# A planner with a pass backwards, a second split third of the last product, a shorter carry chain and one load for the first a

## The chip, the cores and the metric

One Trainium2 chip, one core of it. The metric is device microseconds of one execution, lower is better. A core has TensorE (PE in the rows; PEld is its weight loads), VectorE (DVE), ScalarE (ACT), GpSimd (POOL) and SyncE (SP, which here only issues transfers).

## The reference

Three stages, one after the other. A gated linear attention with a complex decay (batch 4, 8 heads, 768 steps, head size 48), a dense layer with a maximum of three products, and a mixture of 8 experts of which each token takes one:

```python
for t in range(S):
    new_re = ar * S_re - ai * S_im
    new_im = ar * S_im + ai * S_re
    S_re, S_im = (new_re + kv, new_im)
    y[:, :, t] = np.einsum('bhd,bhde->bhe', q[:, :, t], S_re)
...
h = np.maximum(np.maximum(x @ w1, x @ w2), x @ w3)     # 3072 x 384 by 384 x 768
x = h @ w_out                                           # 768 x 384
...
expert_idx = np.argmax(logits, axis=1)                  # logits: normed x by normed embeddings / tau
out[mask] = gate_w[mask, None] * (np.maximum(x[mask] @ w1[e], 0.0) @ w2[e])
```

## The kernel before

The program has two phases. Phase 1 computes attention and the dense layer; phase 2 the experts. The change touches phase 1 only.

**Phase 1** runs over 12 units of 256 tokens. Each unit u goes through: `load_a` (decays, 768 KB), `front` (norms the decays, L438 to L462), `mid` (running products of the decays: 7 steps over the 8 lanes, then the "carry chain" over 8 blocks and 3 groups, with the small tiles `Ct`, `gt`, `G` and `C`, L471 to L513), `back` (scales q and k into `QK` and sends them by 12 transfers `S<-QK` into the tile S, L515 to L564), `attn` for two halves (TensorE: pk, pa, pT, py; L582 to L657) and `moe1` (L769 to L822). A step of `mid` is `cmul_step`: one multiply (`sa`, `sb`, `sc`) and one add, each depending on the one before. `mid` ends with a sign change (`minus`) that the carry chain needs, two memsets into `Ct`, one copy into it, and the same again for `G`.

**moe1** has three thirds f2 = 0, 1, 2. For each, 54 matmuls into three PSUM tiles `ph`, a maximum on VectorE giving `h` (128 x 512), and the last product h by `w_out` into `px`. In thirds below `SPLIT` (1, L1065) h and the weight are split in a high and a low part (`hhi`, `hlo`; `wohi`, `wolo`) and px takes three fp32r matmuls a product; in the others px takes one fp32 matmul, which the trace shows as two instructions. `hhi` has one buffer, the tag "h" (h and hlo) has two.

**Weights** (L660 to L754): 24 pieces of 64-bit weights come through the POOL queue, are turned to fp32 on ScalarE and VectorE and, where they are needed split, split with two ScalarE casts and two matmuls (`pd`). This runs beside the first unit.

**What sets the order.** Every instruction of phase 1 goes through a `Recorder` (L125 to L320), which knows a cost for each and the dependences; `issue` (L247) sorts them by a list schedule: it takes the engine that is free first, and of the instructions that could start within `SLACK` = 120 ns the one with the smallest key, then the longest path behind it. Keys are given by hand (`KEYS`, L1070): a unit's number plus an offset, so that routing (`route_early`, key 10.5) lies between `moe1(10)` (10.3) and `moe1(11)` (11.3). Instructions of one engine run in the order of this plan. All recorded instructions stand at L313 in the trace. The plan also puts filler matmuls (`keep_warm`, L571; trace line L578) ahead of TensorE work where it foresees an idle time over 0.9 us.

**Into phase 2.** `route_early` (L939) chooses experts for the first 20 tiles: VectorE work, two small matmuls `within` in the middle of it, more VectorE work, a table `tab` with the experts of the first blocks; then `first_rows` (L988) gathers the first block's tokens and transposes them. Phase 2 then loads the first expert's weights (`queue_q_buf`, L1177), copies them (`w1s`, L1206) and multiplies (`ph<-xT,w1s`, L1252). None of phase 2 is known to the planner.

Of the kernel before, what the change touches and what calls it, by code (L numbers as in the profile page):

```python
# [31 lines left out]
L = 8  # L32
# [84 lines left out]
class Op:  # L117
    __slots__ = ("eng", "calls", "cost", "preds", "succs", "rank", "n", "start", "end", "dma", "key")

    def __init__(self, eng):  # L120
        self.eng, self.calls, self.cost, self.preds, self.dma = eng, [], 0.0, {}, 0.0
        self.succs, self.key = [], 0.0


class Recorder:  # L125
# [6 lines left out]
    def __init__(self, nc):  # L132
        self.nc = nc
        self.ops = []
        self.hist = {}
        self.slot = {}
        self.before = {}
        self.cur = None
        self.idle = None
        self.lazy = None  # L140
# [49 lines left out]
    def price(self, op, eng, method, out, ins, k):  # L190
        n = out.free_size()
        psum = any(x.space == PSUM for x in ins + [out])
        if "dma" in method:
            op.cost += 1040.0 if eng != "sync" else 460.0 if len(ins[0].shape) < 4 or ins[0].space == bass.MemoryType.DRAM else 625.0
            op.dma = 2000.0 + out.nbytes() / 200.0
        elif eng == "tensor":
            m, r, b = ins[0].free_size(), ins[0].dtype == F32R, ins[0].dtype == BF16
            op.cost += (14.0 if r else 2.5) + (2 * n if method == "transpose" else n if r else max(n, m) if b else 4 * max(n, m)) / 2.4 * (
                0.25 if m <= 32 else 0.6 if m <= 64 else 1.0)
            if m <= 32 and len(op.calls) == 1:  # L200
                op.cost += 250.0
        elif eng == "vector":
            w = 0.5 if method in ("tensor_copy", "tensor_scalar", "memset") and not psum else 8 if method == "reciprocal" else 1
            op.cost += (n * w + 66) / 0.96
        elif eng == "scalar":
            op.cost += (144 if isinstance(k.get("scale"), bass.AP) else 51 if psum else 94) + n / 1.2
            op.cost += 100 * (k.get("accum_out") is not None) + 90 * isinstance(k.get("bias"), bass.AP)
        else:
            op.cost += 150 + n * 2.2 if method in ("tensor_mul", "tensor_sub") else 100 + n / 0.9
# [36 lines left out]

    def issue(self):  # L247
        ops = self.ops
        for i, o in enumerate(ops):
            o.n = len(o.preds)  # L250
            for p, raw in o.preds.items():
                p.succs.append((o, raw))
        done = set()
        for o in reversed(ops):
            o.rank = o.cost + max((self.lat(o, s, raw) + s.rank for s, raw in o.succs), default=0.0)
        free = dict.fromkeys(("vector", "scalar", "tensor", "gpsimd", "sync"), 0.0)
        ready = {e: [] for e in free}
        for o in ops:
            o.start = 0.0
            if o.n == 0:  # L260
                ready[o.eng].append(o)
        left = len(ops)
        for e, x in self.START.items():
            free[e] = x
        pipe = 0.0
# [20 lines left out]
        while left:  # L286
            best = None
            for e, row in ready.items():
                if not row:
                    continue  # L290
                t = max(free[e], min(o.start for o in row))
                if best is None or t < best[0]:
                    best = t, e
            t, e = best
            o = max((o for o in ready[e] if o.start <= t + self.SLACK), key=lambda o: (-o.key, o.rank))
            if o.key == self.lazy:
                o = max((x for x in ready[e] if x.start <= t + 130.0 and x.key < o.key), key=lambda o: (-o.key, o.rank), default=o)
            ready[e].remove(o)
            o.start = max(o.start, t)
            if e == "tensor":  # L300
                x = free[e]
                while self.idle and x > self.IDLE[0] and o.start - x > self.IDLE[1] and self.idle(o):
                    x = hold(x, 2 * 216.0)
                    x += self.IDLE[2] if warm[0] else 50.0
                o.end = free[e] = hold(o.start, o.cost)
            else:
                o.end = free[e] = o.start + o.cost
            if o.dma:

                pipe = max(pipe, o.end) + o.dma - 2000.0  # L310
                o.dma = pipe + 2000.0 - o.end
            for c in o.calls:
                getattr(getattr(self.nc, c[0]), c[1])(*c[2], **c[3])  # L313
            left -= 1
            for s, raw in o.succs:
                s.start = max(s.start, o.end + self.lat(o, s, raw))
                s.n -= 1
                if s.n == 0:
                    ready[s.eng].append(s)
        return max(o.end for o in ops)  # L320

    START = {"gpsimd": 4000.0, "scalar": 2500.0, "sync": 1000.0}
# [5 lines left out]
class Prog:  # L328
# [64 lines left out]
    def consts2(self):  # L393
# [13 lines left out]
        q.sync.dma_start(self.rtau, self.io["tau"].to_broadcast([128, 1]))  # L407
        with self.keyed(self.KEYS["early"]):
            q.vector.reciprocal(self.rtau, self.rtau)
# [54 lines left out]
    def cmul_step(self, out, f, x, shape, tag):  # L464
# [4 lines left out]
        v.tensor_add(out, m[:, 0], m[:, 1])  # L469

    def mid(self, u):  # L471
# [5 lines left out]
        for i in range(1, L):  # L477
            self.cmul_step(X[:, 1:3, i], X[:, 1:3, i - 1], X[:, :, i], [NB], "sa")

        Ct = self.tl(p, [128, 3, NB], "Ct", 1, f"Ct{u}")  # L480
# [7 lines left out]
        minus(tot[:, 0], tot[:, 2], 1)  # L488
# [3 lines left out]
        v.memset(Cg[:, 1, :, 0], 1.0)  # L492
        v.memset(Cg[:, 2, :, 0], 0.0)
        v.tensor_copy(Cg[:, 1:3, :, 1], Tg[:, 1:3, :, 0])
        gt = self.tl(p, [128, 3, 12], "gt", 1, f"gt{u}")
        for i in range(2, 9):
            out = Cg[:, 1:3, :, i] if i < 8 else gt[:, 1:3]
            self.cmul_step(out, Cg[:, 1:3, :, i - 1], Tg[:, :, :, i - 1], [12], "sb")
        minus(gt[:, 0], gt[:, 2], 2)

        G = self.tl(p, [128, 3, 12], "G", 1, f"G{u}")
        G4, g4 = tl(G), tl(gt)
        v.memset(G4[:, 1, :, 0], 1.0)
        v.memset(G4[:, 2, :, 0], 0.0)
        v.tensor_copy(G4[:, 1:3, :, 1], g4[:, 1:3, :, 0])
        for i in range(2, 4):
            self.cmul_step(G4[:, 1:3, :, i], G4[:, 1:3, :, i - 1], g4[:, :, :, i - 1], [3], "sc")
# [492 lines left out]
    def phase1(self):  # L1000
        nc, tc = self.nc, self.tc
        with ExitStack() as ctx:
# [25 lines left out]
            self.X, self.S, self.QKr, self.xt, self.C = {}, {}, {}, {}, {}  # L1028
            K = self.KEYS
# [4 lines left out]
            self.q.lazy = self.q.key if self.LAZY else None  # L1034
# [4 lines left out]
            for u in range(NU):  # L1039
# [9 lines left out]
                if u + 2 < NU:  # L1049
                    self.load_a(u + 2)  # L1050
                self.q.key = u + K["attn"]
# [13 lines left out]
    SPLIT = 1  # L1065
# [3 lines left out]
    LAZY = False  # L1069
# [632 lines left out]
```

## Time and profile before

| | us |
|---|---|
| three runs | 827.15, 832.43, 832.0 |
| median | 832.0 |
| the profiled execution | 830.61 |
| its span from first to last instruction | 828.7 |
| busy in the span: PE / PEld / DVE / ACT / POOL | 763.0 / 690.1 / 631.5 / 439.3 / 136.3 |

The profile is of one execution. The page gives busy shares per engine and per slice of the span; the windows view gives busy time of each engine in chosen stretches with the granted TensorE clock (1.00 is 2.4 GHz, 0.5 would be 1.2 GHz); the timeline lists instructions by start; a bracket at its end says how long the engine sat idle before and what ended that. Busy time of PE is modelled: matmuls overlap, so the pace is read from starts, not from durations.

### The profile page before, as it was taken

The page shows a single profiled execution, that of the slowest core. Times are in us where ns is not written, and L with a number is a line of the kernel's source. Part 1 is how long each engine was busy: PE and PEld are TensorE (multiplying, and loading weights), DVE is VectorE, ACT ScalarE, POOL GpSimd, SP SyncE. Part 2 cuts the span into 40 slices and gives each one's busy share as a digit, 9 for nine tenths or more (in the row PEclk, how much of TensorE's full clock was granted, in tenths as well). Part 3 has the DMA queues.
Part 4 walks back from the last instruction along what each step waited for, and adds up shares of the span by engine and source line. Part 5 has one row for each costly group of instructions (what it writes and reads, how often), then busy time and mean ns, then how long its engine had stood idle before and what let it go on. Part 6 is the DMA issues. An engine that isn't in the chain of part 4 may idle for free. (4 is left out here: it accounts for less than half of the span.)

```text
span 828.7 us, 19402 instructions
## 1 busy us (share of the span) xinstructions
PE 763.0 (92%) x7709; PEld 690.1 (83%) x7709; DVE 631.5 (76%) x1299; ACT 439.3 (53%) x944; POOL 136.3 (16%) x193
## 2 busy tenths in 40 slices
PE   1677789999999999999999999999969999999996
PEld 0565679889898989889897989889958999989886
DVE  4998989999999999999999844539976545556431
ACT  8998745545656545565355521128254556545521
POOL 5331101010200102010100100021023213223111
PEclk9999999999999999999999999999998999999998
DMA  8705070626437170725346140060046795773500
GB/s 306 287 14 142 13 162 15 184 68 129 126 72 171 37 183 30 167 94 104 111 85 149 33 96 2 20 214 26 30 154 236 245 401 186 257 278 119 184 22 24
DMA packets 38612, 107.21 MB, mean 129 GB/s; under 512 B 5460, under 2 KB 27011, under 8 KB 35440
## 3 DMA queue, kind: packets, MB, share of 16 engines
q1 hardware_dynamic: 30032, 77.15, 32.0%
q0 software_dynamic: 7936, 27.94, 10.4%
q8 instruction: 62, 1.02, 0.5%
q10 hardware_dynamic: 544, 0.79, 0.3%
q14 instruction: 38, 0.31, 0.1%
HBM read 96.35 MB, written 10.62 MB: 129 GB/s over the span
## 5 line engine op out<-in xcount | busy, mean ns | idle before, releaser
L313 PE MATMUL ph<-xhi,whi 128*128 128x256 f32 x648 | 121.6, 296 | 0.2 <-DVE h L313 0.2
L313 PE MATMUL ph<-xhi,wlo 128*128 128x256 f32 x648 | 112.8, 283 | 0.0
L313 PE MATMUL ph<-xlo,whi 128*128 128x256 f32 x648 | 112.8, 283 | 0.0
L313 PEld LDWEIGHTS ph<-xhi,whi 128*128 128x128 f32 x648 | 93.5, 191 | 7.0 <-issue 2.0
L313 PEld LDWEIGHTS ph<-xlo,whi 128*128 128x128 f32 x648 | 93.0, 191 | 0.0
L313 PEld LDWEIGHTS ph<-xhi,wlo 128*128 128x128 f32 x648 | 92.9, 191 | 0.0
L1252 PE MATMUL ph<-xh,w1s 128*128 128x256 f32 x264 | 77.1, 292 | 0.0
L1214 DVE TENSOR_TENSOR w2l<-queue_q_buf,w2h 128x768 fp32r<-128x768 f32 x52 | 47.6, 954 | 38.0 <-ACT w2h L1213 37.9
L1252 PE MATMUL ph<-xh,w1l 128*128 128x256 f32 x264 | 74.7, 283 | 0.0
L1252 PE MATMUL ph<-xl,w1s 128*128 128x256 f32 x264 | 74.7, 283 | 0.0
L313 DVE TENSOR_TENSOR h<-ph,h 128x512 f32<-128x512 f32 x72 | 49.4, 687 | 29.7 <-PE ph L313 29.4
L1268 PE MATMUL py<-w2h,hlo 128*128 128x384 f32 x200 | 68.2, 342 | 3.1 <-DVE hlo L1257 3.1
L1268 PE MATMUL py<-w2h,hhi 128*128 128x384 f32 x200 | 69.2, 346 | 0.0
L1268 PE MATMUL py<-w2l,hhi 128*128 128x384 f32 x200 | 67.9, 339 | 0.0
L313 PE MATMUL px<-wo,h 128*128 128x392 f32 x192 | 67.7, 496 | 0.0
L1257 DVE SCALAR_TENSOR_TENSOR hlo<-ph,hhi 128x512 fp32r<-128x512 f32 x50 | 34.3, 686 | 30.5 <-ACT hhi L1256 30.4
L313 POOL COPY QK<-X 128x6 f32<-128x6 f32 x24 | 29.2, 1246 | 168.1 <-DVE X L313 141.2
L1256 ACT ACTIVATE hhi<-ph 128x512 fp32r<-128x512 f32 x50 | 29.9, 598 | 50.6 <-PE ph L1252 48.8
L313 PEld LDWEIGHTS px<-wo,h 128*128 128x128 f32 x192 | 35.2, 190 | 22.6 <-issue 2.0
L1252 PEld LDWEIGHTS ph<-xh,w1s 128*128 128x128 f32 x264 | 50.5, 191 | 3.8 <-issue 3.1
L313 PE MATMUL pa<-S 112*128 112x128 f32 x384 | 52.2, 279 | 0.2 <-DVE G L313 0.2
L1252 PEld LDWEIGHTS ph<-xh,w1l 128*128 128x128 f32 x264 | 50.5, 191 | 0.5
(401 smaller groups left out, 1796.7 us busy)
## 6 DMA issues: line engine op xcount, KB each, us to landing
queue_q_buf<-w SPq DMA_DIRECT2D x26, 1536.0 KB
S<-QK SPq DMA_DIRECT2D x46, 289.1 KB
QKr<-qk SPq DMA_DIRECT2D x11, 768.0 KB
X<-a SPq DMA_DIRECT2D x10, 768.0 KB
w1m<-w SPq DMA_DIRECT2D x5, 1536.0 KB
w2m<-w SPq DMA_DIRECT2D x5, 1536.0 KB
v<-v POOLq DMA_DIRECT2D x24, 224.0 KB, 2.9
x1d<-x1s SPq DMA_DIRECT2D x20, 192.0 KB
```

The lines of the kernel that those rows point to most:

```text
L313: getattr(getattr(self.nc, c[0]), c[1])(*c[2], **c[3])
L1214: v.tensor_sub(lo, bv[:, c], hi.bitcast(F32))
L1252: t.matmul(ph[:, f], a, b, start=o == 0, stop=o == len(ops) - 1)
L1256: s.activation(hi, ph, AF.Relu).ins,
L1257: v.scalar_tensor_tensor(lo, ph, 0.0, hi.bitcast(F32), op0=ALU.max, op1=ALU.subtract).ins]
L1268: t.matmul(py, a[:, f, r], c[:, k % 4], start=o == 0, stop=o == 3 * KF - 1)
```

## The change

- The planner. `issue` first makes a plan by keys as before (with two small corrections, `BIAS`, for the routing embedding's VectorE work and for the matmuls of `pa`). Then up to four times: `backward` places all instructions from the end back, with the same costs, and so gets a latest start for each; `forward` makes a new plan that always takes the instruction with the smallest latest start, among those that can start within `WAIT` = 130 ns. A new plan is kept only if its modelled end is over 1 ns earlier. The plans assume TensorE at its full clock; only the filler matmuls still use the clock model. Costs: an issue of a transfer by POOL 600 instead of 1040 ns, transfers out of DRAM at 380 instead of 200 bytes/ns, POOL begins at 2200 instead of 4000 ns.
- `SPLIT` 2 instead of 1: two of the three thirds of the last product are split; four of the six `w_out` pieces are kept split instead of two.
- The carry chain: `Ct` and `G` are made once, with their constant ones and zeros, not per unit; the copies into `Ct` and `G` go to ScalarE; the first step reads the source of the copy; the sign change after the last lane is made from the step's products, not from its sum.
- `load_a(0)`: one transfer instead of three. `front(0)` still works in three cuts.
- The load of tau and its reciprocal are recorded after the first unit's loads, not among the constants (the attribute `behind` that is set around it is read nowhere).

```diff
+    def forward(self, first, wait):
...
+            t, e = min((max(free[e], min(start[i] for i in row)), k, e) for k, (e, row) in enumerate(ready.items()) if row)[::2]
+            row = ready[e]
+            c = min((i for i in row if start[i] <= t + wait), key=lambda i: first[i])
+            if wait > self.SLACK:
+                b, c = c, min((i for i in row if start[i] <= t), key=lambda i: first[i])
+                x = start[b]
+                if b != c and max(t - first[c], t + ops[c].cost - first[b]) > max(x - first[b], x + ops[b].cost - first[c]):
+                    c = b
...
+    def backward(self, start, end, land, seq):
+        ops, n, last = self.ops, [len(x) for x in self.after], max(end)
+        late, by = [0.0] * len(ops), [last] * len(ops)
...
+            c = max((i for i in row if by[i] >= t - 1.0), key=lambda i: end[i])
+            row.remove(c)
+            late[c] = free[e] = min(by[c], t) - ops[c].cost
+            for j, x in self.back[c]:
+                by[j] = min(by[j], late[c] - (land[j] - end[j] + 150.0 if x is None else x))
...
+        for _ in range(self.PASSES):
+            x = self.forward(self.backward(*plan), self.WAIT)
+            if max(x[1]) >= max(plan[1]) - 1.0:
+                break
+            plan = x
...
-        for c in self.cuts(u):
-            (e or self.q.sync).dma_start(X[:, 1:3, c], self.io["a"][u][:, :, c])
+        (e or self.q.sync).dma_start(X[:, 1:3], self.io["a"][u])
...
+        if neg is not None:
+            v.scalar_tensor_tensor(neg, m[:, 0, 1], -1.0, m[:, 1, 1], op0=ALU.mult, op1=ALU.subtract)
...
-        minus(tot[:, 0], tot[:, 2], 1)
...
-        v.memset(Cg[:, 1, :, 0], 1.0)
-        v.memset(Cg[:, 2, :, 0], 0.0)
-        v.tensor_copy(Cg[:, 1:3, :, 1], Tg[:, 1:3, :, 0])
+        self.q.scalar.copy(Cg[:, 1:3, :, 1], Tg[:, 1:3, :, 0])
...
-    SPLIT = 1
+    SPLIT = 2
```

## Rows read from the trace of the kernel before

**Rows 1.** Windows: stretch, length, busy us (instructions) of each engine, clock, DMA share, GB/s.

```profile
0.00:111.20 111.20, 67.16 (x526) 52.92 (x526) 94.83 (x229) 92.37 (x210) 34.01 (x82) 0.94 0.47 153
111.20:480.00 368.80, 367.76 (x4618) 332.77 (x4618) 349.67 (x719) 197.84 (x492) 35.82 (x50) 1.00 0.43 104
```

**Rows 2.** Timeline of TensorE, first attention to first dense product: start, us, what, count.

```profile
84.34 0.55 PE L313 MATMUL pk<-ident,S 112*128 112x112 f32 x4
...
107.31 3.21 PE L578 MATMUL pT<-ident 128*64 128x128 f32 x15 [4.78 <-ACT M L313]
...
111.21 0.62 PE L313 MATMUL ph<-xhi,whi 128*128 128x256 f32 x3
```

**Rows 3.** Timeline of TensorE, end of unit 10 to phase 2.

```profile
516.77 0.34 PE L313 MATMUL px<-wohi,hhi 128*128 128x392 f32 x1
516.95 0.34 PE L313 MATMUL px<-wolo,hhi 128*128 128x392 f32 x1
...
522.14 5.43 PE L313 MATMUL px<-wo,h 128*128 128x392 f32 x16
527.40 0.44 PE L313 MATMUL within<-oneh,ones 128*128 128x160 f32 x2
...
551.10 5.43 PE L313 MATMUL px<-wo,h 128*128 128x392 f32 x16
```

**Rows 4.** Groups by line and form: operation, shapes, count, busy us, mean ns, idle before.

```profile
L313 PEld LDWEIGHTS px<-wo,h 128*128 128x128 f32 x192 | 35.2, 190 | 22.6 <-issue 2.0 <-DVE Ct L313 0.2
L313 PEld LDWEIGHTS px<-wohi,hhi 128*128 128x128 f32 x48 | 9.0, 189 | 0.4 <-issue 0.4
L313 DVE TENSOR_TENSOR hlo<-h,hhi 128x512 fp32r<-128x512 f32 x12 | 8.3, 688 | 1.1 <-ACT hhi L313 1.0
L313 ACT CAST hhi<-h 128x512 fp32r<-128x512 f32 x12 | 7.4, 618 | 21.8 <-DVE h L313 21.7
L313 ACT ACTIVATE fy<-X 128x768 f32<-128x768 f32 x11 | 9.3, 844 | 0.8 <-DMA X<-a 0.8
```

**Rows 5.** The tile Ct: instructions that write it, ns min/median/max, first and last start.

```profile
L313 DVE MEMSET Ct<- x24: 68/68/68, 0.9 to 434.6; 128x12 f32 x24
L313 DVE COPY Ct<-X x12: 181/185/194, 26.8 to 452.7; 128x24 f32<-128x24 f32 x12
```

**Rows 6.** Timeline of VectorE: front(0), carry chain and end of unit 0, carry chain of unit 1.

```profile
10.51 0.16 DVE L313 RECIPROCAL rtau<-rtau 128x1 f32<-128x1 f32 x1 [3.38 <-DMA rtau<-tau]
...
26.70 0.21 DVE L313 TENSOR_SCALAR X<-X 128x96 f32<-128x96 f32 x1
...
41.94 0.36 DVE L313 TENSOR_TENSOR C<-mc 128x192 f32<-128x192 f32 x1
...
60.42 1.82 DVE L313 TENSOR_TENSOR QK<-rr,X 128x768 f32<-128x768 f32 x2
...
80.40 0.21 DVE L313 TENSOR_SCALAR X<-X 128x96 f32<-128x96 f32 x1
...
86.26 0.36 DVE L313 TENSOR_TENSOR C<-mc 128x192 f32<-128x192 f32 x1
```

**Rows 7.** Timeline of ScalarE: the wait for the third cut of a.

```profile
8.85 0.44 ACT L313 ACTIVATE fy<-X 128x288 f32<-128x288 f32 x1 [1.52 <-DMA X<-a]
```

**Rows 8.** Timeline of SP: transfers it issues; the time is that of the issues.

```profile
62.33 0.33 SPq L313 DMA_DIRECT2D X<-a  x1
62.71 9.17 SPq L313 DMA_DIRECT2D S<-QK  x6
...
441.03 11.66 SPq L313 DMA_DIRECT2D S<-QK  x12
...
543.95 0.36 SPq L1177 DMA_DIRECT2D queue_q_buf<-w  x1
```

**Rows 9.** Timeline of VectorE at the boundary, and of TensorE behind it.

```profile
553.06 3.41 DVE L1206 COPY w1s<-queue_q_buf 128x1536 f32 x2 [1.07 <-DMA xg<-x1d,srcrow]
...
556.69 8.21 PE L1252 MATMUL ph<-xT,w1s 128*128 128x128 f32 x72
```

More of the change, by code (lines that the diff above doesn't have):

```diff
@@ L117 @@
 class Op:
[L118 removed]
+    __slots__ = ("eng", "calls", "cost", "preds", "dma", "key")
     def __init__(self, eng):
         self.eng, self.calls, self.cost, self.preds, self.dma = eng, [], 0.0, {}, 0.0
[L122 removed]
+        self.key = 0.0
 class Recorder:
@@ L245, in lat, with kind @@
         return self.LAT + self.FROM[p.eng] + (60.0 if o.eng == "tensor" else 0.0)
-    def issue(self):
[L248 to L265, printed above, removed]
+    def kind(self, op):
+        c = op.calls[0]
+        x = c[2][0] if c[2] else c[3]["out"]
+        name = getattr(x, "ap", x).tensor.name if type(x) is bass.IndirectOffsetOnAxis else x.tensor.name
+        return "".join(c for c in name.rstrip("0123456789").rstrip("_") if not c.isdigit())[:4] + op.eng[0]
@@ new lines, in forward @@
+    def forward(self, first, wait):
+        ops, n = self.ops, [len(x) for x in self.back]
+        start, end, land, seq = [0.0] * len(ops), [0.0] * len(ops), [0.0] * len(ops), []
+        free = {e: self.START.get(e, 0.0) for e in self.ENGINES}
+        ready = {e: [i for i, o in enumerate(ops) if o.eng == e and n[i] == 0] for e in free}
+        pipe = 0.0
+        while len(seq) < len(ops):
+            t, e = min((max(free[e], min(start[i] for i in row)), k, e) for k, (e, row) in enumerate(ready.items()) if row)[::2]
[7 more added lines that the diff above has]
+            row.remove(c)
+            o = ops[c]
+            start[c] = max(start[c], t)
+            end[c] = free[e] = start[c] + o.cost
+            seq.append(c)
+            if o.dma:
+                pipe = max(pipe, end[c]) + o.dma - 2000.0
+                land[c] = pipe + 2000.0
+            for j, x in self.after[c]:
+                start[j] = max(start[j], land[c] + 150.0 if x is None else end[c] + x)
+                n[j] -= 1
+                if n[j] == 0:
+                    ready[ops[j].eng].append(j)
+        return start, end, land, seq
@@ L266, in issue @@
+    def issue(self):
+        rank = self.graph()
+        plan = self.forward([(o.key + self.BIAS.get(self.kind(o), 0.0), -rank[i]) for i, o in enumerate(self.ops)], self.SLACK)
+        for _ in range(self.PASSES):
[3 more added lines that the diff above has]
+            plan = x
+        start, end, _, seq = plan
         busy, warm, seen = {}, [False], [0]
@@ L285, in hold @@
             return end
[L286 to L311, printed above, removed]
+        free = 0.0
+        for i in seq:
+            o = self.ops[i]
+            if o.eng == "tensor":
+                while self.idle and free > self.IDLE[0] and start[i] - free > self.IDLE[1] and self.idle(o):
+                    free = hold(free, 2 * 216.0)
+                    free += self.IDLE[2] if warm[0] else 50.0
+                free = hold(max(start[i], free), o.cost)
             for c in o.calls:
                 getattr(getattr(self.nc, c[0]), c[1])(*c[2], **c[3])
[L314 to L322, printed above, removed]
+        return max(end)
+    ENGINES = "vector", "scalar", "tensor", "gpsimd", "sync"
+    BIAS = {"embv": 0.33, "pa_t": 0.25}
+    PASSES, WAIT = 4, 130.0
+    START = {"gpsimd": 2200.0, "scalar": 2500.0, "sync": 1000.0}
     WINDOW = 4096 / 1.2
@@ L1050, in phase1 @@
                     self.load_a(u + 2)
+                if u == 0:
+                    self.q.behind = [o for o in self.q.ops[-2 * len(PIECES) - 8:] if o.dma]
+                    self.q.sync.dma_start(self.rtau, self.io["tau"].to_broadcast([128, 1]))
+                    self.q.behind = []
+                    with self.keyed(K["early"]):
+                        self.q.vector.reciprocal(self.rtau, self.rtau)
                 self.q.key = u + K["attn"]
```

54 lines of the change are left out of this document (37 added, 17 removed).

## The prediction

> **What bounds the kernel now.** I read the page's slices first, then the windows, then the timelines at the three places where the windows change. Phase 1 has two regimes. From 111.2 us on TensorE is full: 367.8 us busy of 368.8, weight loads 332.8 [rows 1]. VectorE beside it shows 349.7, but its busy time counts the latency of dependent small steps, so it has some slack. Before 111.2 TensorE shows 67.2 of 111.2, and much of that is weight conversion and filler; VectorE has 94.8 and ScalarE 92.4 [rows 1]. The first dense product waits until 111.21 [rows 2]; call this moment T0. From T0 to the last product of phase 1, which begins at 551.10 and lasts 5.43 [rows 3], TensorE works through a backlog without a hole. So a microsecond taken off T0, or off TensorE's work behind it, comes off the end of phase 1, as long as VectorE keeps feeding. The reader should also see the seam: phase 2's first matmul starts at 556.69, when the second of two copies of 3.41 us in all that began at 553.06 is done [rows 9]. TensorE's end and the weights' arrival coincide there within half a microsecond; neither has slack.
>
> **Part by part.**
>
> *Second split third.* Both forms are in the trace. The fp32 form issues 16 instructions for two thirds from 522.14 until `within` starts at 527.40, 0.33 us each [rows 3], 8 of them a third: 2.63 us. The split form starts one every 0.18 [rows 3], 12 a third: 2.14 us. Saved: 0.49 us a unit, 5.9 us over 12 units, all behind T0 and so on the path. The price is one cast of 618 ns on ScalarE and one subtraction of 688 ns on VectorE a unit [rows 4]. ScalarE is busy 197.8 of 368.8 [rows 1] and takes it. VectorE's 0.69 is paid by the next edit. The split product now waits for cast and subtraction; the 54 `ph` matmuls of the last third stand between and hide about 1.5 us. If that cover is gone, 1.5 us a unit, 18 us: I exclude it because the first third already lives this way [rows 3]. The one buffer of hhi and the two of "h" are turned over more often; bounds 0 to 3 us, I take 0 here and put it into the feed below.
>
> By weight loads alone the sum would be another one: 8 loads of 190 ns a third become 12 of 189 [rows 4], +0.75 us a unit, +9.0 in all. The starts 0.18 apart, closer than one load lasts, show that loads do not set the pace [rows 3, 4]. The Trainium skill ("Perfetto Trace Analysis", Identifying the Most-Contended Engine) judges TensorE by the busy share of weight loads, not of matmuls; by that rule this edit would cost. The trace disagrees, so the rule is only a small rival.
>
> Two more weight pieces are split before T0: four casts, at most 0.62 each [rows 4], 2.5 us of ScalarE.
>
> *Carry chain.* Per unit VectorE loses four memsets (68 ns for Ct's) and two copies (185 for Ct's) [rows 5], about 0.6 us; the sign change only moves off the chain. With the 0.69 added VectorE is even. The copies on ScalarE are needed only at the end of the chain; if ScalarE is late there, up to 0.3 us a unit, inside the feed term.
>
> *First a and tau.* The third cut of a came at 8.85, ScalarE having waited 1.52 [rows 7]; VectorE stood 3.38 us behind tau's reciprocal at 10.51 [rows 6]. One transfer means the first cut waits for all of a, at worst until 8.85, still ahead of the 10.51 at which VectorE got on. The tau stall goes if the reciprocal is planned late. Bounds -3.4 to +1; I take -2.5 on T0. Kept by keys, tau's load (now key -1) would be issued ahead of a's (key 0): one more issue of 0.33 [rows 8].
>
> *Order.* This is the large term and no row shows the new order, so I bound T0 from both sides. Along the path: unit 0's carry chain took 26.70 to 42.30, because conversions of half a microsecond stood between its steps; unit 1's, alone, took 80.40 to 86.62 [rows 6]. With the 130 ns wait and latest times the critical unit gets the second form: 15.6 less 6.2, less the removed copies and sign change of 0.5, is 9.9 us. With the 2.5 above T0 is 98.8. The filler of 3.2 us at 107.31 [rows 2] stood where the plan foresaw idleness, and the load of a later a, issued at 62.33 on SP just ahead of unit 0's six S transfers [rows 8], need not be there: 92 to 96 without them. By supply: ScalarE did 92.4 us before T0, of which two later fronts, 16 instructions of 0.844 [rows 4], 13.5, need not come first; 92.4 - 13.5 + 2.5 = 81.4. Never idle, that ends at 82; at its share so far (0.83) at 98. I take 93, 18 us earlier, nearer the share that was kept than the full one; 82 and 103 bound it.
>
> *Feed.* With an earlier T0 VectorE's lead shrinks. Unit 1's QK can end where TensorE has only unit 0's dense product as backlog. Bounds 0 and 9 us (0.8 a unit); I take 3.
>
> *Seam.* `within` ran at 527.40, directly behind unit 10's last product [rows 3], because key 10.5 put it there. From it to the load of the expert's weights (543.95 [rows 8]) 16.6 us pass, and from there to the first matmul 12.7 [rows 9], 29.3 in all: just the length of unit 11's dense layer. The planner knows nothing of the 12.7. By latest times alone `within` need only run some 17 us before the end; ties go by the plan before, which speaks for its old place. Bounds 0 and 12 us of idle TensorE; I take 5.
>
> Sum against the profiled execution: 830.6 - 5.9 - 18 + 3 + 5 = 814.7, 815. The three runs' median is 1.4 above the profiled one; within their spread, so I leave 815.
>
> **Rivals.**
>
> *T0 moves further and the seam holds* (T0 82, feed 0, seam 0): 830.6 - 5.9 - 29 = 796. For it: unit 0's chain has much slack to lose; against: ScalarE would have to run without a gap.
>
> *The new order gives nothing* (no later plan is better by the model, or the chip does not follow it): -5.9, -2.5, seam 0 to 5: 822 to 827, 825. For it: before T0 VectorE was busy 85% [rows 1].
>
> *S comes just in time, and late: slower.* The plan still costs an S transfer 0.625 us on SP, 7.5 for twelve; the trace has 11.66 [rows 8]. A plan that works to latest times may send S 4.2 us later than TensorE needs it. It decides where TensorE's other work has run out when S is due. In half of 11 units +23: 838; in all +46: 861. For it: VectorE no longer runs far ahead by keys; against: it is not idle while work is ready, and in the old plan its lead grew.
>
> *Loads bound TensorE:* 814.7 + 14.9 = 830; the 0.18 speaks against it.
>
> **Chances.** Forecast 815 (804 to 823): 0.47. 796 (790 to 804): 0.12. No use of the order, 825 (822 to 830): 0.20. S late, 838 (828 to 861): 0.19. Loads: 0.02. From 799 to 838 leaves out about 0.07 below and 0.09 above. One per cent of 832.0, about what a measurement of this kernel can tell from no change, puts the limits at 823.7 and 840.3: faster 0.46 + 0.12 + 0.04 = 0.62, slower 0.09 or so from late S, 0.10; within 0.28.
>
> **What would show it.** Split: a unit has 8 fp32 px instructions instead of 16 and 24 split ones instead of 12, 0.18 apart. Order: first `ph<-xhi,whi` at 85 to 103 and unit 0's carry chain in about 6 us. Tau: no stall at the start of VectorE. Feed: TensorE's idle time between T0 and the last product, named after `S<-QK` or `at` if it grows. Seam: `within` less than 29 us before the last px, and TensorE idle between it and `ph<-xT,w1s`. I am wrong in the main point if T0 stays above 105, or if it falls and the last px does not come earlier by as much.

## The result, and the profile of the changed kernel

The changed kernel takes 834.97 us (median of 20 runs) against 830.05 of the kernel before (20 runs beside them): a ratio of 1.0066, 95% interval 1.0047 to 1.0086. It is slower by two thirds of a per cent; 815 was forecast. The profiled execution has a span of 833.5 us, the one of before 828.7. In the experiments below, three executions of e2 and one each of e8 and e10 fell in a slower state; the ratios leave them out, and without them the medians are 831.56, 851.64 and 829.55.

The windows view of the changed kernel, cut at its first dense product (T0) and at its last `px`; columns as in [rows 1]:

```profile
0.00:98.50 98.50, 57.28 (x486) 45.98 (x486) 85.93 (x205) 86.30 (x198) 27.33 (x82) 0.90 0.47 162
98.50:556.50 458.00, 443.48 (x5373) 411.01 (x5373) 388.49 (x774) 229.58 (x583) 32.39 (x55) 1.00 0.41 94
```

The same stretch of the kernel before, from its T0 to its last `px`:

```profile
111.20:556.50 445.30, 443.47 (x5313) 400.42 (x5313) 382.64 (x808) 212.49 (x530) 40.96 (x55) 1.00 0.41 101
```

T0 came 12.7 us earlier, and the first phase ends at 556.5 all the same. TensorE stands idle for 458.00 - 443.48 = 14.5 us behind T0; before it was 445.30 - 443.47 = 1.8. What it waited for is in the view of waits (us in all, times, longest). All rows of TensorE over that stretch of the changed kernel, then the first one of before:

```profile
PE pk L357 <- DMA S<-QK: 11.1, 12, 1.9
PE ph L357 <- DVE h L357: 1.7, 2, 1.4
PE pa L357 <- DVE at L357: 1.6, 1, 1.6
```

```profile
PE pk L313 <- DMA S<-QK: 1.0, 3, 0.5
```

`pk` transposes a unit's S; it is the first thing TensorE does with it. Unit 7 in the timelines of SP and of TensorE:

```profile
330.84 0.33 SPq L357 DMA_DIRECT2D X<-a  x1
331.26 13.24 SPq L357 DMA_DIRECT2D S<-QK  x12
...
343.52 0.80 PE L357 MATMUL pk<-ident,S 112*128 112x112 f32 x4
345.25 0.45 PE L357 MATMUL pk<-ident,S 112*128 112x112 f32 x3
346.06 0.29 PE L357 MATMUL pk<-ident,S 112*128 112x112 f32 x1 [0.36 <-DMA S<-QK]
```

Four of these transposes take 0.55 when nothing is missing [rows 2]; 0.80 and the bracket are TensorE standing at S. Everything behind them in its queue stands too.

A wait can also cost more than its idle time. Behind the longest of them the granted clock of TensorE falls to its lower level, 1.2 GHz, though TensorE works without a gap again; the wait, and a window of 1 us behind it:

```profile
453.77 0.29 PE L357 MATMUL pk<-ident,S 112*128 112x112 f32 x1 [1.95 <-DMA S<-QK]
...
455.00:456.00 1.00, 1.00 (x7) 1.00 (x6) 0.92 (x3) 0.82 (x3) 0.00 (x0) 0.50 0.36 58
```

In the windows from 455 to 458 the clock is 0.50, and at 459 it is 1.00 again; some 1.7 us of TensorE's work are lost (an estimate, from the clock and the busy time of each window). The kernel before has 1.00 in every such window from T0 to the last `px`.

The second loss is the seam. TensorE, SP and VectorE around the end of the first phase, against [rows 3, 8, 9]:

```profile
541.56 0.27 PE L357 MATMUL pxg<-ident,xg 128*128 128x128 f32 x1
542.75 0.27 PE L357 MATMUL pxg<-ident,xg 128*128 128x128 f32 x1
554.93 0.27 PE L357 MATMUL pxg<-ident,xg 128*128 128x128 f32 x1
...
555.41 0.36 SPq L1220 DMA_DIRECT2D queue_q_buf<-w  x1
...
562.35 3.41 DVE L1249 COPY w1s<-queue_q_buf 128x1536 f32 x2 [0.47 <-DMA queue_q_buf<-w]
...
565.93 0.42 PE L1295 MATMUL ph<-xT,w1s 128*128 128x128 f32 x1
```

The third transpose of the first gathered rows is held back to 554.93. SP's load of the expert's weights waits for it (row `SPq L1220 <- PE pxg L357: 14.2` of the waits), goes out at 555.41 instead of 543.95 [rows 8], and phase 2 starts multiplying at 565.93 instead of 556.69 [rows 9]: 9.2 us. Here too the clock falls while TensorE stands, and the first products of phase 2 run at about half speed, some 2.5 us more (an estimate: 0.45 of 5.57):

```profile
565.93:571.50 5.57, 5.57 (x30) 5.57 (x30) 2.60 (x14) 0.69 (x2) 0.00 (x0) 0.55 0.18 69
```

The ledger to the span: T0 -12.7, idle TensorE +12.7, seam +9.2, and the way from the first `ph<-xT,w1s` to the end 267.6 instead of 272.0, -4.4. Sum +4.8, the span's difference. The 4.4 hold the 2.5 us at the lower clock already. Phase 2 gives most of this back where TensorE waits for gathered rows in either kernel: 7.35 and 0.83 us at 622 to 625 before, 4.15 at 631 after; that the rows had more time to come is the likely reason and was not tested. TensorE's busy time did not fall by the split's 5.9; that is taken up below.

### The profile page after: what moved, and what is told of

It is laid out like the page before. It is cut to its first block, busy times and chain, and to the rows that moved or that the text cites. A ratio compares the mean times of both kernels' runs of the same rounds, so it can differ in the third digit from the quotient of the medians.

```text
span 833.5 us, 19446 instructions
## 1 busy us (share of the span) xinstructions
PE 756.2 (91%) x7727; PEld 696.6 (84%) x7727; DVE 631.9 (76%) x1243; ACT 450.5 (54%) x984; POOL 122.0 (15%) x193
## 5 line engine op out<-in xcount | busy, mean ns | idle before, releaser
L357 PE MATMUL ph<-xhi,whi 128*128 128x256 f32 x648 | 122.8, 298 | 1.7 <-DVE h L357 1.7
L357 PE MATMUL ph<-xlo,whi 128*128 128x256 f32 x648 | 112.8, 283 | 0.0
L357 PE MATMUL ph<-xhi,wlo 128*128 128x256 f32 x648 | 112.8, 283 | 0.0
L357 PEld LDWEIGHTS ph<-xhi,whi 128*128 128x128 f32 x648 | 94.5, 191 | 10.9 <-issue 3.8
L357 PEld LDWEIGHTS ph<-xlo,whi 128*128 128x128 f32 x648 | 93.1, 191 | 0.0
L357 PEld LDWEIGHTS ph<-xhi,wlo 128*128 128x128 f32 x648 | 93.1, 191 | 0.0
L357 DVE TENSOR_TENSOR h<-ph,h 128x512 f32<-128x512 f32 x72 | 49.4, 686 | 24.5 <-PE ph L357 23.6
L357 PE MATMUL pa<-S 112*128 112x128 f32 x384 | 50.8, 278 | 2.0 <-DVE at L357 1.6
L357 POOL DMA_DIRECT2D v<-v x24 | 13.0, 541 | 259.6 <-PE py L357 258.5
L1295 PEld LDWEIGHTS ph<-xl,w1s 128*128 128x128 f32 x264 | 50.6, 192 | 0.0
L357 PEld LDWEIGHTS pa<-S 112*128 112x128 f32 x384 | 47.5, 193 | 2.9 <-DVE at L357 1.8
```

Source lines behind the costliest of these rows:

```text
L1295: t.matmul(ph[:, f], a, b, start=o == 0, stop=o == len(ops) - 1)
```

## The experiments

All kernels are the changed one with the edit named (e6: the kernel before). Every edit of the plan sorts the whole first phase anew, so two runs differ by more than the edit's own place. The stages are therefore read by T0, by TensorE's idle time behind it (length less busy time of the window from T0 to the last `px`), and by its waits for S; of e2 the table has only the time, since its profiled execution took 837.09 us, 5 above its median. The stage columns are of one profiled execution, the time is the median of all. In most runs the two lie within 3.1 us of each other; the profiled execution of e4 is 5.7 faster, those of e7 and e9 are 8.1 and 7.2 slower. The 21.7 us of waits for S that the expectations of e9 and e13 name (and e1 by its parts) add rows of matmuls (9.1) and of weight loads (4.1 and 8.5), which overlap; the table counts matmuls alone. "The plan's end" in the expectations is what the kernel's own planner holds for phase 1.

| run | T0 | idle T0 to last px | of it, pk for S | last px | us | ratio to before, 95% |
|---|---|---|---|---|---|---|
| before | 111.2 | 1.8 | 1.0 | 556.5 | 830.05 | |
| changed | 98.5 | 14.5 | 11.1 | 556.5 | 834.97 | 1.0047 to 1.0086 |
| e1 | 108.0 | 6.2 | 2.2 | 554.1 | 835.65 | 1.0044 to 1.0090 |
| e2 | | | | | 831.92 | 0.9978 to 1.0034 |
| e3 | 109.1 | 6.0 | 1.5 | 556.3 | 829.99 | 0.9972 to 1.0017 |
| e4 | 97.8 | 22.8 | 4.7 | 570.3 | 847.71 | 1.0177 to 1.0259 |
| e5 | 98.7 | 17.0 | 8.6 | 561.9 | 838.31 | 1.0058 to 1.0124 |
| e6 | 106.1 | 3.9 | 2.4 | 553.0 | 826.28 | 0.9930 to 0.9967 |
| e7 | 106.7 | 20.2 | 7.3 | 575.4 | 839.52 | 1.0075 to 1.0136 |
| e8 | 107.8 | 22.3 | 10.3 | 578.5 | 852.23 | 1.0206 to 1.0278 |
| e9 | 104.7 | 17.8 | 7.5 | 573.5 | 846.25 | 1.0162 to 1.0225 |
| e10 | 104.1 | 12.8 | 4.8 | 558.5 | 830.38 | 0.9973 to 1.0027 |
| e11 | 116.7 | 4.1 | 0 | 558.4 | 828.69 | 0.9956 to 0.9993 |
| e12 | 102.1 | 18.1 | 16.3 | 572.0 | 852.33 | 1.0235 to 1.0294 |
| e13 | 101.9 | 9.8 | 0 | 557.4 | 831.24 | 0.9980 to 1.0014 |
| e14 | 101.5 | 3.9 | 0 | 544.6 | 818.30 | 0.9829 to 0.9873 |
| e15 | 102.4 | 6.7 | 0 | 549.4 | 823.94 | 0.9903 to 0.9949 |
| e16 | 108.5 | 7.1 | 0 | 561.6 | 834.80 | 1.0004 to 1.0058 |
| e17 | 108.8 | 15.3 | 13.2 | 570.3 | 842.59 | 1.0124 to 1.0175 |
| e18 | 94.4 | 12.8 | 0 | 552.2 | 826.56 | 0.9934 to 0.9979 |

**The seam: e1 to e3.** e1 changes a price, `else 625.0` for a send of S to `970.0`; e2 the backward pass, which now counts the early route (keys 9.5 and 10.5) from `TAIL` = 12700 ns before the end; e3 is both.

```diff
-        late, by = [0.0] * len(ops), [last] * len(ops)
+        late, by = [0.0] * len(ops), [last - self.TAIL * (o.key in (9.5, 10.5)) for o in ops]
```

> The changed kernel with one number of the planner altered: an S transfer on SP is priced 970 ns instead of 625 (12 of them took 12.1 and 12.3 us in the changed kernel's trace, the plan holds 7.5). The plan's own end moves from 534.0 to 541.2 us. Theory A (the gain of phase 1 was lost because S lands later than the order assumes, and TensorE's queue stands at the transposes of S): in 125 to 480 us the waits of TensorE for S, 9.1 + 4.1 us by DMA and 8.5 by issue in the changed kernel, fall to under 6 in sum, the last px product ends at 545 to 550 instead of 556.4, and the time is 825 to 830. Rival (the feed of VectorE and ScalarE, or the backward order itself, loses it): the waits move to other rows, the last px product ends at 554 or later, and the time is 833 to 840.

> The changed kernel with the backward pass counting the early route and the first gathered rows from 12.7 us before the plan's end, so that the last transpose of these rows is not put at the end of phase 1. The last px product stays where it was, 555 to 557. Theory B (the 9.6 us between the last px product and the first product of phase 2 come from that transpose, since SP's load of the queue waits for it): the third transpose runs before 546, the first product on w1s starts at 556.5 to 559 instead of 565.9, and the time falls by 5 to 9 us, to 826 to 830. Rival (the gather of the late route sets phase 2, so an earlier start only makes TensorE wait longer there): the first product starts early too, but the gap between 600 and 640 us grows by the same, and the time is 832 to 836.

> Both edits together: S transfers at 970 ns in the plan, and the early route counted from 12.7 us earlier. Theories A and B: last px product at 545 to 550, first product on w1s within 3 us of it, time 815 to 823, faster than both kernels. If only B holds: 826 to 830. If neither: 833 to 838.

e1 and e3 end the first phase alike (554.1, 556.3). Behind it e1 needs 9.1 us to the first `ph<-xT,w1s`, and e3 none: its third transpose is at 542.59, and the timeline of TensorE goes on

```profile
556.10 0.49 PE L1272 MATMUL pxg<-ident,xg 128*128 128x128 f32 x3
556.43 1.84 PE L1295 MATMUL ph<-xT,w1s 128*128 128x128 f32 x15
```

From there to the end it takes 270.3 instead of 267.6 us: a third of the seam is lost again at the gather (7.04 and 1.07 us at 622 to 625), as the rival said in part. Net: 835.65 to 829.99, 5.7 us; e2 alone 3.4 by the medians, 5 by the ratios (1.0066 to 1.0006). So the seam is shown. Theory A is not: e1's waits for S fell to 2.2 us, but T0 moved back by 9.5 and nothing was gained.

**The order by keys: e4.** `PASSES, WAIT = 0, 130.0`.

> The changed kernel with no backward pass (PASSES 0): the first stage in the order of the hand-given keys, with all the other edits kept. The plan's own end is 549.2 us instead of 534.0. Theory A: the keys leave S more ahead of its use, so TensorE waits for S in 125 to 480 us for under 8 us, and the chip follows the plan closer than the 22 us of the changed kernel; the last px product ends at 556 to 562 and the last transpose of the first rows runs early as in the kernel before, so the time is 825 to 833. Rival (the passes are worth what the plan says, and the loss lies in split or feed): the last px product ends 12 to 15 us later than in the changed kernel, at 568 or more, and the time is 838 to 848.

The rival's numbers came. The passes are worth some 13 us to this kernel, on the chip too (847.71 to 834.97).

**VectorE: e5 to e8.** From 20 to 450 us VectorE is busy for 95% in either kernel (windows view: 409 of 430 us before, 408 after). If it set the pace of S, relieving it would help. e5 and e6 leave two operations a unit out.

```diff
-        v.tensor_mul(m2, m2, y2)
-
-        v.scalar_tensor_tensor(y, m2, 3.0, y, op0=ALU.subtract, op1=ALU.mult)
-
-        s.activation(m2, y, AF.Copy, scale=-0.5 * 0.999)
-        s.activation(y2, y, AF.Identity, scale=0.5e-6, bias=self.one)
+        s.activation(m2, y, AF.Copy, scale=0.999)
+        s.activation(y2, y, AF.Identity, scale=-1.0e-6, bias=self.one)
```

> The changed kernel without the Newton step on the reciprocal root of the input's scale (it leaves out that part of the computation): two VectorE operations of 0.95 us each fewer per unit, 1.9 us of some 36 us of VectorE work per unit; nothing of TensorE's work changes. Theory C (VectorE, 95 to 97 per cent busy from 20 to 450 us in every kernel so far, sets the pace at which S is ready, so TensorE's gains of 12.7 + 5.9 us can't be used): the S sends of units 5 to 11 start 6 to 15 us earlier than in the changed kernel, the last px product ends at 540 to 547 instead of 556.4, and the time falls by 9 to 16 us, to 819 to 826. Rival A (it is only the order, with S sent too late by the plan's price): at most 4 us, 831 or more.

> The kernel before without the same Newton step, the same two VectorE operations of 0.95 us per unit. TensorE has 3 us of holes from the first dense product on there, so by theory C it is the bound and VectorE just keeps up: only the way to the first dense product gets shorter, 2 to 5 us, the last px product ends at 551 to 555, and the time is 825 to 828. If VectorE alone set the pace of the kernel before too, the gain would be as large as in the changed kernel, 9 us or more.

e6 came as expected (T0 5.1 us earlier, where 2 to 5 were expected). e5 did not. S did go out earlier, for unit 7 at 319.03 instead of 331.26, and TensorE waited for it just the same (SP, then TensorE, of e5):

```profile
319.03 15.07 SPq L357 DMA_DIRECT2D S<-QK  x12
...
330.63 0.45 PE L357 MATMUL pk<-ident,S 112*128 112x112 f32 x3
333.63 0.29 PE L357 MATMUL pk<-ident,S 112*128 112x112 f32 x1 [2.54 <-DMA S<-QK]
```

That speaks against theory C: S went out 12 us earlier, the order asked for it earlier too, 11.6 us after its first send, and the last `px` came later (561.9), not earlier. This wait is made by the order; VectorE was relieved and it stayed.

e7 puts 42 ns on each VectorE operation in the plan (`(n * w + 66)` to `(n * w + 106)`) and e1's and e2's edits; e8 moves `QKr * R` and `m2 * y2` to GpSimd beside that.

> The changed kernel with the planner told what the traces show: 42 ns more for each VectorE operation, 970 ns for an S transfer, and the early route counted from 12.7 us earlier. The work is the same; by these prices the plan's own end is 561.0 us instead of 534.0, which is near the chip's 556.4. Theory C: no order is much better, the last px product ends at 552 to 560 and the time is 828 to 833. Rival A (the wrong prices made a bad order): the last px product ends before 548, the time is below 824.

> As the run before it, and two multiplications of 768 columns per unit moved from VectorE to GpSimd (QKr by R, and the one of the Newton step), 1.9 us per unit of VectorE's time, with the computation unchanged. The plan's end falls from 561.0 to 543.2 us. Theory C: the last px product ends at 540 to 548 and the time is 815 to 823, faster than both kernels. Against it: GpSimd may take far longer for them than the plan's 1.84 us and hold up the chain to S, or slow VectorE down while both run; then the mean of VectorE's groups rises and the time is 828 or more.

e7 missed both its cases, and in e8 the case against theory C came. The 42 ns were a mistake of reading: busy time counts overlapping ends. Two operations of 0.95 each stand in one row with 1.82 [rows 6], so one costs 0.87 of the queue, which the plan had right. With this price too high the order got worse: e7 is e3 with the 42 ns, 839.52 for 829.99. e8 adds two measured things (groups by form of GpSimd and of VectorE):

```profile
L357 POOL TENSOR_TENSOR QKr<-QKr,rr 128x768 f32<-128x768 f32 x12 | 34.2, 2850 | 19.2 <-ACT rr L357 17.4 <-issue 1.7
...
L357 DVE TENSOR_TENSOR m<-X,C 128x768 f32<-128x768 f32 x48 | 48.0, 1023 | 4.3 <-ACT C L357 4.2
```

The multiplication takes 2.85 us there, three times VectorE's, on the chain to S (the other one 1.94). VectorE's own `m` rose from 0.95 to 1.02, its `X<-m` to 1.08 and its `rr` to 1.50; `QK` stayed at 0.95.

**Sending S: e9 and e12, e10.** e9 is e2 with `BOTH = 12`, e12 is e9 with `SPLIT = 1`, e10 is e3 with 1120 for 970.

> The changed kernel with the early route counted from 12.7 us earlier (as in e2) and one more constant altered: the half of the S transfers that GpSimd issues for unit 0 is issued by GpSimd for every unit (BOTH 12 instead of 1), 6 by SP and 6 by GpSimd. All prices of the plan stay; VectorE's and TensorE's work is the same. Theory A (S arrives later than the order assumes because SP needs 12 to 14 us for 12 sends, where the plan holds 7.5): the sends of a unit take 6 to 9 us, TensorE's waits for S in 125 to 480 us fall from 21.7 us (9.1 + 4.1 by DMA, 8.5 by issue) to under 6, the last px product ends at 544 to 551 instead of 556.4, and the time is 816 to 824. Rival C (VectorE and ScalarE feed the products no faster, whatever S does): the waits go to other rows, the last px product ends at 554 or later, and the time is 829 or more.

> As e9, with the split of the last product undone (SPLIT 1 as in the kernel before). TensorE's work on px grows by 6.4 us (88.7 us in the kernel before, 82.3 in the changed one), VectorE loses 12 operations hlo<-h,hhi of 0.68 us, 8.2 us over the stage, and ScalarE 12 of hhi. If TensorE is the bound once S is early: the last px product ends 4 to 7 us later than in e9. If VectorE's load counts as much: within 2 us of e9, either way.

> As e3, with the price of an S transfer on SP at 1,120 ns instead of 970, so that the plan's 12 sends take 13.4 us where the traces show 12 to 14.5. Nothing else differs from the changed kernel but the early route counted from 12.7 us earlier. Theory A (the price alone made the order bad; with a price that is not below the chip's, the order keeps a margin): TensorE's waits for S under 4 us in 125 to 480 us, last px product at 546 to 552, time 818 to 826. Rival C: as e3 or worse, last px product at 554 or later, 829 or more.

e9 and e10 missed theory A's numbers, and the rival's came; the last `px` of e12 lies within 2 us of e9's, its second case. e9 says why theory A fails. Unit 7 of e9, by the timelines of SP, GpSimd and TensorE and by a window:

```profile
340.35 0.33 SPq L357 DMA_DIRECT2D X<-a  x1
340.78 9.14 SPq L357 DMA_DIRECT2D S<-QK  x6
...
340.85 3.33 POOL L357 DMA_DIRECT2D S<-QK  x6 [1.67 <-DVE QK L357]
...
354.84 1.39 PE L357 MATMUL pk<-ident,S 112*128 112x112 f32 x8 [0.92 <-DMA S<-QK]
...
341.00:355.00 14.00, 13.08 (x86) 11.06 (x86) 13.04 (x30) 10.33 (x30) 3.18 (x6) 1.00 0.93 198
```

GpSimd is done with its sends at 344.2 and SP with its own at 349.9, but TensorE still waits for S at 354.8, 14 us after the first send. Over the units where TensorE waits, S is there 12.2 to 15.2 us after the first send in e9, and 11.7 to 15.1 in the changed kernel. In unit 7 the 16 DMA engines are, from 341 to 355, 93% busy and move 198 GB/s: the rest of the load of a (768 KB, issued just ahead), the 1.54 MB of S, two stores of x1. So SP's 12 to 14 us for twelve sends were for the most part back-pressure from busy DMA engines, not the price of a send. Where little is under way, SP needs some 0.6 us for one. In the kernel before, the first two sends of a unit, and two single ones late in another:

```profile
149.41 1.29 SPq L313 DMA_DIRECT2D S<-QK  x2
...
270.63 0.61 SPq L313 DMA_DIRECT2D S<-QK  x1
...
272.03 0.60 SPq L313 DMA_DIRECT2D S<-QK  x1
```

Nor does it take a load of a: units 10 and 11 of the changed kernel have none ahead, and their twelve sends take 12.13 and 12.33 us. The Trainium skill ("DMA: Bandwidth & Descriptors", Issuing engines are not separate DMA queues) says that transfers of all issuing engines run on the same 16 DMA engines; e9's row agrees. So S came no sooner than before, and the waits for it stayed: 7.5 us in e9, 16.3 in e12. e9's and e12's TensorE is also busy for longer, 450.99 and 451.77 us from T0 to the last `px`. Most of that is the clock. In e9 it falls to 0.50 four times, each time at an idle time of TensorE (1.88 us before 156.78 for `h`, 2.92 before 242.18 for S, 4.06 before 269.36, 1.80 before 506.02 for S); one such stretch:

```profile
243.00:247.00 4.00, 4.00 (x23) 4.00 (x23) 3.40 (x4) 3.97 (x9) 1.92 (x2) 0.57 0.09 31
```

Added up over windows of 1 us from T0 to the last `px` (estimates, as above), the work lost at the lower clock is 7.4 us in e9 and 7.6 in e17, 5.0 in e7, 6.2 in e8, 3.0 to 3.4 in e4, e5, e12 and e13, 1.6 to 1.7 in the changed kernel, e10, e16 and e18, and nothing in the kernel before, e1, e3, e6, e11, e14 and e15. e12 also lacks the split's 5.9, so that this pair does not price the split. An order with long waits pays for some of them twice. Not every wait does this: behind the 1.72 us before 304.92 in the changed kernel the clock stays at 1.00.

**The rates: e11, e13 to e15.** The change had made loads from DRAM faster in the plan. All transfers share one pipe there, so S, queued behind the load of a, was planned to land earlier too. e11 undoes that line, e13 slows S's own rate instead. These two and the two after them have e2's edit as well.

```diff
-            op.dma = 2000.0 + out.nbytes() / (380.0 if ins[0].space == bass.MemoryType.DRAM else 200.0)
+            op.dma = 2000.0 + out.nbytes() / 200.0                                                        # e11
+            op.dma = 2000.0 + out.nbytes() / (380.0 if ins[0].space == bass.MemoryType.DRAM else 125.0)   # e13
```

e14: 300 and 125, a send of S 800, `LAT = 180.0`, `PASSES, WAIT = 6, 100.0`; e15: 300 and 132, the last of these too.

> The changed kernel with the early route counted from 12.7 us earlier and one line of the change undone: loads from DRAM are again priced at 200 bytes per ns in the plan instead of 380, which puts the planned landing of S 9 to 10 us behind its last send in the middle units (4.4 in the changed kernel's plan) since all transfers share one pipe there. The plan's own end is 546.0 us instead of 534.0. Theory A in its narrow form (the margin that this price had given by accident is what was lost): TensorE's waits for S under 6 us in 125 to 480 us, first dense product at 106 to 114, last px product at 549 to 555, time 823 to 830. Rival: the last px product ends at 556 or later and the time is 831 or more.

> The changed kernel with the early route counted from 12.7 us earlier and one number altered in the plan: transfers within SBUF at 125 bytes per ns instead of 200, so that the 1.54 MB of a unit's S take 12.3 us of the plan's pipe and land 16.7 us after the first send; e9 showed 12 to 14.5 us from the first send to the first use, whichever engines sent. All other prices and all work stay. Theory A2 (the transfer itself, not SP's issuing, takes 12 to 14 us, and the order is bad where it holds less): TensorE's waits for S in 125 to 480 us fall from 21.7 us to under 5, the first dense product at 98 to 106, the last px product at 545 to 552, the time 817 to 825. Rival C (VectorE's and ScalarE's feed bounds the stage at what all runs so far had): waits move to other rows, the last px product ends at 554 to 560, the time is 826 to 834.

> As e13, and with more margin in the plan: loads from DRAM at 300 bytes per ns (380 before), a send on SP at 800 ns (625), 180 ns instead of 100 for a signal between engines, and the passes without their look-ahead (WAIT 100). The plan's own end is 539.0 us. Theory A2: as e13 or better, the last px product ends at 543 to 550, the time is 815 to 823. Rival C: 554 to 560 and 826 to 834.

> As e13 with 132 bytes per ns within SBUF, 300 from DRAM, and WAIT 100; SP's price and the signal's time as in the changed kernel. The plan's own end is 536.2 us. Theory A2: the last px product ends at 543 to 550, the time is 815 to 823. Rival C: 554 to 560 and 826 to 834.

In all four no row of TensorE waiting for S is left; e2, from which e11 and e13 differ by one line each, has 12.7 us of them in its profiled execution. How that comes about is seen at unit 7 of e14 (SP, then TensorE):

```profile
319.35 13.68 SPq L357 DMA_DIRECT2D S<-QK  x12
...
336.17 0.55 PE L357 MATMUL pk<-ident,S 112*128 112x112 f32 x4
```

The sends take as long as ever, but the order now puts the first `pk` 16.8 us behind the first send, where the changed kernel had 12.3 (343.52 - 331.26) and S came after 14.8.

e14 met all its numbers, e15 all but the time (823.94 for at most 823). e11 met waits and time, not T0 (116.7 for at most 114) and last `px` (558.4 for at most 555). e13 is a miss, where rival C's numbers came: the waits went to VectorE and ScalarE, and 28 filler products stand in its queue. So the waits for S go with the rates, but the time need not: by the ratios e13 is where e2 is (0.9997 and 1.0006), e11 0.3% faster than e2, e15 0.8 and e14 1.6, the last two with the plan's other margins moved as well. The windows from T0 to the last `px` of e11 and of e14:

```profile
116.70:558.40 441.70, 437.62 (x5367) 407.81 (x5366) 386.88 (x770) 222.54 (x560) 36.70 (x55) 1.00 0.43 100
```

```profile
101.50:544.60 443.10, 439.23 (x5363) 408.50 (x5362) 381.69 (x762) 222.76 (x579) 47.15 (x55) 1.00 0.44 100
```

e11 shows the other side of the old price: S has a margin again, but T0 is later than in any other run, at 116.7.

**Rates or other margins: e16 to e18.** e17 is e14 with 380, 200 and 625 back; e18 with `LAT = 100.0`; e16 with `SPLIT = 1`.

> As e14, but with the three rates of the changed kernel back in the plan (380 bytes per ns from DRAM, 200 within SBUF, 625 ns for a send of S); the 180 ns for a signal between engines and WAIT 100 stay. The plan's own end is 541.1 us. Theory A2 (the rates of the transfers are what spoiled the order): the waits of TensorE for S come back, 10 us or more in 125 to 480 us, the last px product ends at 554 to 562, the time is 828 to 836. Rival D (the signal's time and the missing look-ahead made e14 good, not the rates): the last px product ends below 549, the time is below 823.

> As e14 with 100 ns for a signal between engines as in the changed kernel; the rates and WAIT 100 stay. The plan's own end is 539.8 us. Theory A2: no waits for S, first dense product at 98 to 105, the last px product at 545 to 550, the time 818 to 824. Rival D: 553 or later, 827 or more.

> As e14 (818.3 us, last px product at 544.6) with the split of the last product undone (SPLIT 1), planned anew with the same prices. TensorE's own work on px is 6.4 us more (88.7 against 82.3 us in the kernels before and after), VectorE's 12 operations of 0.68 us on hlo fewer. If the order has no waits for S, TensorE is the bound of the stage and the split is worth about what it takes from TensorE: the last px product ends at 549 to 553 and the time is 823 to 827. If VectorE bounds it as much: at 546 or earlier, 820 or less.

e17 settles that these three prices matter: they are 24.3 us between e14 and e17, more than expected (some 7.6 of it at the lower clock, by the estimate above), and the waits for S are back (the row below). Which of the three does it is not in e17; e1 and e10 had a dearer send and still waited for S, e11, e13 and e15 had slower rates with the send at 625 and did not.

```profile
PE pk L357 <- DMA S<-QK: 13.2, 10, 3.0
```

e18 has no waits for S, but 12.8 us of others (3.2 at one `pa` for `at`, 2.6 for `h`), and missed its numbers by 2 to 4 us, T0 to the early side: beside the rates, the longer signal is worth 8 us. e16 missed: its TensorE was busy 445.99 us from T0 on against 439.23, 6.8 more, of which 1.7 at the lower clock; the 5.1 left stand against 6.4 expected of the split. But T0 fell back by 7 and idle time grew by 3.

## Why the prediction was wrong, point by point

- **What bounds the kernel.** "A microsecond taken off T0 ... comes off the end of phase 1, as long as VectorE keeps feeding." The condition was the weak place, and S, not VectorE, broke it. In e14, with slower transfers and more margin in the plan, the sentence holds: T0 is 9.7 us before the old one, TensorE is busy 4.2 less behind it and idle 2.0 more, and the last `px` is 11.9 earlier.
- **T0.** Taken at 93 with bounds 82 and 103; measured 98.5, so -12.7 for -18. ScalarE is busy 19.75 and 19.53 of 20 us in 60 to 80 and 80 to 100, which points to the supply as the bound that held, and not the path; the longest wait ahead of fillers is 2.81 us for ScalarE's split weights, at 94.18. The path's sum, 98.8, agrees with 98.5 by luck: it took 9.9 us off unit 0's carry chain, which went from 23.75 to 36.6, 12.8 us instead of about 6, so that 2.8 came off; conversions still stand between its steps. The tau stall was not removed: the reciprocal stands at 6.68 behind a wait of 4.47 us. It seems to cost nothing: VectorE next waits for weights, until 10.28.
- **Split.** -5.9 predicted. e11 against before shows it clean: TensorE busy 437.62 for 443.47, 5.9 less, and e16 against e14 5.1. In the changed kernel it is hidden: TensorE's busy time there contains the waits inside `pk` (0.80 for 0.55 above; all `pk` 22.0 for 19.4 in e11), 3 conversions that fell behind T0 (1.4), and the 1.7 us lost at the lower clock, a little of which is in `pk` too. That is some 5 of the 5.9. The rival by weight loads foresaw that they rise, and they did, 407.81 for 400.42, while TensorE's time fell. The Trainium skill ("Perfetto Trace Analysis", Identifying the Most-Contended Engine) takes the busy share of weight loads, beside the share of peak arithmetic, as the measure of how near TensorE is to its limit. Read like that it agrees with the trace, 407.81 of 441.70 us in e11 for 400.42 of 445.30 before; that more loads mean more time was the prediction's own step.
- **Feed.** The step that failed: 3 us with bounds 0 and 9, measured 12.7, of which 10.1 before `pk`. I had bounded it by VectorE's lead. The quantity that mattered, how long before its use S goes out, was in no term of the forecast but only in a rival: in unit 7 the first `pk` stands 12.3 us behind the first send, and S is there after 14.8. The clock, which falls behind such waits, was in no term either. Of the 20.5 us between the forecast's 814.7 and the profiled 835.2, this term makes 9.7, T0 5.3, and the split's 5.9, used up by waits inside `pk`, conversions and clock, about the rest; the seam came out even.
- **Seam.** +5 predicted, +9.2 at the place and +4.8 net. The mechanism was right (the planner knows nothing of the 12.7 us of phase 2), the instruction was not: `within` was not held back (521), the third transpose was. That the net came so close to 5 is partly luck: phase 2 gave back 4.4 that the prediction did not count on.
- **The rival that came true.** "S comes just in time, and late", 838, given 0.19, was the right case and close to the time. Its reason was half right. The plan does hold too little for S, but twelve sends at 0.625 us are not it: e1 and e10 changed that price and the loss came back in other forms, and e9 halved SP's sends and the landing stayed. It is the rate of the transfers, which the change itself had raised for loads from DRAM: e11 and e13, each with one rate lowered against e2, have no wait for S, and e2 has 12.7 us. That edit was named in the text ahead of the prediction, among the costs, and the prediction prices it nowhere; there lay the clue.

**What stays open.** e13, e16 and e18 have no waits for S and still idle 7 to 13 us, for `at` (VectorE's masked copy of `pa`), `h`, `xhi` (the high part of the dense layer's input). Which of the plan's other prices makes these was not tried. e14 is one good order; that its margins are the best was not looked for.

**A kernel that beats both.** e14: 818.30 us, 0.9851 of the kernel before (0.9829 to 0.9873), with the change's own ideas and other prices in its plan.

## What to carry to other kernels

When an order is computed from prices, an optimiser that places work as late as allowed turns what a price lacks into idle time of the engine whose queue stands, 11.1 us here. A price that is too high is not free either: e7 lost 9.5 us against e3. And an idle time can cost twice, when the clock falls behind it. Before trusting such a change, compare in the trace, for each transfer that the bound engine waits for, the time from first send to landing with what the plan holds, and look at every price that the change touches, even those for other transfers in the same pipe. The planned end of a stage also needs what comes behind it: work that the plan does not know is work it will delay.

## What the runs showed of the hardware

Sending by two engines did not bring data sooner, within the spread of the units (11.7 to 15.1 us from first send to S with one engine, 12.2 to 15.2 with two). In unit 7 S was there 14.8 us after its first send when SP took 13.24 us over twelve sends (DMA engines 87% busy from 331 to 346, 183 GB/s), and 14.1 when SP and GpSimd took 9.14 and 3.33 us over six each (93%, 198 GB/s). A long row of sends on SP is then a sign of busy DMA engines, not of dear sends: two alone took 0.61 and 0.60. A multiplication of 128 x 768 took 2.85 us on GpSimd where VectorE takes 0.95, and VectorE's `m`, of the same size, got 7% longer beside it.

TensorE's granted clock fell to 0.50 (1.2 GHz) behind idle times within the busy stage: 1.95 us at 453.77 in the changed kernel, after which it was 1.00 again by 459, and at the seam, where the 5.57 us from 565.93 on had 0.55. Behind 1.72 us at 304.92 it did not fall.
